# Pins, load order and an operand's copy at three places of a one-core attention and routing kernel

## The chip, the cores and the metric

The kernel runs on one core of one Trainium2 chip. The metric is the device time of one execution in microseconds (us). Several executions were timed, and one more was taken with the hardware profiler; the profile shows the span of that execution on the core, which is a little shorter than its device time.

## The reference

Two blocks follow each other. The first is a linear attention with product features, for 4 batches, 4 heads, 1088 positions and a head dimension of 32:

```python
def phi(x):
    a = np.einsum('rd,bhsd->bhsr', S1, x)
    b = np.einsum('rd,bhsd->bhsr', S2, x)
    return np.einsum('bhsi,bhsj->bhsij', a, b).reshape(*x.shape[:-1], r * r)
q_p, k_p = (phi(q), phi(k))
num = np.einsum('bhsf,bhfd->bhsd', q_p, np.einsum('bhsf,bhsd->bhfd', k_p, v))
den = np.einsum('bhsf,bhf->bhs', q_p, np.sum(k_p, axis=2))[..., None] + 1e-06
x = num / den            # to (4352, 128): all batches and positions, all heads
```

The second sends x (4352 tokens of 128) through 8 experts, weighted by a balanced routing matrix:

```python
P = np.exp(x @ w_gate - max)
for _ in range(8):
    P /= P.sum(1, keepdims=True) + 1e-09
    P /= P.sum(0, keepdims=True) + 1e-09
    P *= N / E
for e in range(E):
    out += P[:, e:e + 1] * (np.maximum(x @ w1[e], 0.0) @ w2[e])   # F = 1024
```

All arithmetic is in float32.

## The kernel before, in words

The experts' products are nearly all of the work, and they keep TensorE (PE) busy from the first tokens on. The program lists the work as items, each an expert `e` on a group of tokens. An item is cut into blocks, and each block has first products (x by W1, L1136 or, in the later form, L1302), a relu on ScalarE (ACT), sums on VectorE (DVE) and second products (relu by W2, L1590). Sums of operands replace some products: early items use seven products where eight would be needed (`seven`, L1215), and from item `first_new` on ("new" items) the first products use sums of x halves and W1 halves and the second ones use twenty products for four blocks (`twenty`, L1265).

Four stages follow one another.

- Up to about 115 us the attention of batches 0 to 3 runs. Early expert products are put between its steps (`fill`, L1702). For each batch `over` (L542) leaves a result in a tile `xt`, and `take_over` (L553) moves it: one transfer into a DRAM tile `xd` (L556) and four from there into `xT`, the tokens for the experts (L558). For the last batch it is called twice: L626 moves columns 0 to 192 over the POOL queue, L641 the rest over the SP queue. `logits` (L566) is the first that needs all of x.
- Beside it and beside the routing, `forms_ahead` (L267) prepares two forms of W1 for each later expert in DRAM tiles `wl` and `wf`: loads over SP (L265, L279), sign changes on ACT (L282, written in place in `turn`), sums by accumulating transfers over POOL (L276) and stores over SP (L279). Every transfer of it is pinned with `keep_in_program_order`.
- The routing (L668) runs to about 175 us. Then comes the turn to the new items: `join_halves` (L860) sums x halves by transfers over POOL (L865), `raw_second` (L803) loads W2 for the first new item, `first_weights` (L787) fetches the forms of W1 over SP (L793), and `make_second` builds the forms of W2 (`ws`, L238 on DVE, L241 on ACT).
- 68 blocks of new items (34 items of two) follow, one every 8.83 us, then the last group of seven-product items and the final sums (`last_part`, L979) with their stores (L1080).

What sets the order. The blocks `tc.manual_schedule` at L1710, L1734 and L1764 hold the named engines in the order in which the program is written: DVE, PE and ACT in the first and third, DVE and PE in the second. SP and POOL are not named, so their instructions are put in order by a scheduler at compile time, by when each is expected to be ready. `keep_in_program_order` ties one instruction behind the one written before it on the same engine. The attention stands in the block of L1734, the routing and everything later in that of L1764.

The order around the turn is written by hand: `TAIL` (L1599) names for each step of the last two old items what is called there. The tiles of W1 and W2 forms come from rings of two buffers with the tags "w1" and "w2" (`wpool`, L77), and the halves in `first_second_forms` (L778) from the ring "y" of a pool that is opened at L1771. In `first_product` (L1307) `wf` is taken as a list of two halves where `loaded_w` holds one. A dictionary `second_forms` decides in `first_weights` whether both forms are fetched or the first alone:

```python
if j in second_forms:
    parts = (0,)
...
if j in second_forms:
    loaded_w[j].append(second_forms[j])
```

At the very end `last_products` (L1245) gives the order of the last second products: products p2 and p4 of the last eight blocks were held back in `held`, and one product `(both, f, 2, 0, 0)` adds the upper and the lower half of the tile `f`, a copy of the sum s0, into the sum s2. `last_part` makes that copy when s0 is done (`k == 0`).

Of the kernel before, what the change touches and what calls it, by code (L numbers as in the profile page):

```python
# [44 lines left out]
def kernel(  # L45
# [12 lines left out]
    nc = tc.nc  # L58
    P = nc.NUM_PARTITIONS
    B, H, S, D = q.shape  # L60
# [58 lines left out]
    xT = big.tile([P, N + 2 * 32], F32, name="xT")  # L119

    W9 = 9 * 32
# [231 lines left out]
    both = consts.tile([P, H2], F32, name="both")  # L353
# [186 lines left out]
    turned = {}  # L540
# [11 lines left out]

    def take_over(b, lo, hi, queue):  # L553

        xd = dram.tile([P, H, hi - lo], F32, name=f"xd{b}{lo}")
        queue.dma_start(out=xd, in_=turned[b][:, :, lo:hi])  # L556
        for h in range(H):
            queue.dma_start(  # L558
                out=xT[32 * h:32 * (h + 1), b * S:b * S + 4 * W9].rearrange("d (f n) -> d f n", f=4)[:, :, lo:hi],
                in_=xd.rearrange("(f d) h n -> h d f n", f=4)[h])  # L560

    def logits(c):
        lo, hi = chunks[c]
# [38 lines left out]
    def attention(b):  # L602
# [22 lines left out]
        if b + 1 == B:  # L625
            take_over(b, 0, 192, nc.gpsimd)  # L626
# [9 lines left out]
        if b + 1 < B:  # L636
            take_over(b, 0, W9, nc.gpsimd)
            if b + 2 == B:
                forms_of_two()
        else:  # L640
            take_over(b, 192, W9, nc.sync)  # L641
# [226 lines left out]
    first_new = first_weighted  # L868
# [38 lines left out]
    def put(y, lo, n, queues):  # L907
        b0, nb = lo // 32, n // 32
        yt = pools[0].tile([P, NT3 // 32, 32], F32, tag="yt", name="yt", bufs=3)[:, 0:nb, :]
        nc.vector.transpose(out=yt.rearrange("p b d -> p (b d)"), in_=y)  # L910
        store(yt, b0, b0 + nb, queues)

    def part(g, k):

        if g in DIRECT:
            lo, n, _, es, _ = groups[g]
            nc.scalar.copy(kept[es[0]][:, lo + k * n:lo + (k + 1) * n], sums[g][k])
        elif groups[g][2] == 3 or PLAIN - 2 <= g < PLAIN:
            ended[k] = g
        elif g < len(groups) - 1:  # L920
            part_of_seven(g, k)
        else:
            last_part(g, k)
# [47 lines left out]
    def last_rooms(g):  # L971
        n = groups[g][1]
        own = parts.setdefault(g, {})
        if not own:
            own.update(y=[room("m")[:, n * t:n * (t + 1)] for t in range(2)],
                       **{a: room(a, n) for a in "zwxfr"})
        return [own[a] for a in "yzwxfr"]

    def last_part(g, k):  # L979


        lo, n, *_ = groups[g]
        s0, s1, s2, s3 = sums[g]

        def add(out, a, b):
            nc.vector.tensor_tensor(out, a, b, op=Alu.add)

        (y1, y2), z, w, x, f, r = last_rooms(g)
        if k == 3:
            nc.scalar.copy(r[upper], s3[lower])  # L990
            add(w[upper], s3[upper], r[upper])
        elif k == 0:
            nc.scalar.copy(z[upper], s0[lower])
            nc.scalar.copy(f, s0)
            add(x[upper], z[upper], w[upper])
            add(z[upper], x[upper], s0[upper])
        elif k == 2:
            nc.scalar.copy(r[lower], s2[upper])
            nc.scalar.copy(x[lower], s0[lower])
            add(y2[upper], z[upper], s2[upper])  # L1000
            add(y2[lower], s2[lower], r[lower])
            add(x[upper], x[upper], s2[upper])
            put(y2, lo + n, n, (nc.sync, nc.scalar))
        else:
            add(y1, s1, x)
            put(y1, lo, n, (nc.sync, nc.scalar))
# [175 lines left out]
    two_ = pqg[:, 0:2]  # L1182
# [32 lines left out]
    def seven(k):  # L1215

        j, q = blocks[k]
        _, w2, ws = loaded_w[j]
        h, ts, _ = hs[k]
        lo, hi = slice(0, H2), slice(H2, DM)  # L1220
        p1 = (w2[:, 2 * q, lo], h[0], 0, 0, 0)

        five, six = (0, 2) if weighted_of(k) else (2, 0)
        p6 = (ws[:, 1, q], ts[2], six, 1, 0)
        p2 = (w2[:, 2 * q + 1, lo], h[2], 1, 0, 0)
        p4 = (w2[:, 2 * q + 1, hi], ts[3], 1, 1, 0)
        p3 = (ws[:, 3, q], h[3], 2, 0, 0)
        p5 = (ws[:, 0, q], ts[0], five, 1, 0)
        p7 = (ws[:, 2, q], ts[1], 3, k % 2, 0)
        bank0 = [p1, p5] if five == 0 else [p1, p6]  # L1230
        bank2 = [p3, p6] if six == 2 else [p3, p5]
        if k >= len(blocks) - HELD:
            held.append([(k, p2), (k, p4)])
            if k == len(blocks) - 2:
                return bank0, bank2, [p7]
            if k == len(blocks) - 1:
                return [p7, p1], [p5, p3], [p6]
            return (bank0, bank2, [], [p7]) if k % 2 == 0 else (bank0[::-1], bank2[::-1], [], [p7])
        if k % 2 == 0:
            return bank0, [p2, p4], bank2, [p7]  # L1240
        return bank0[::-1], [p4, p2], bank2[::-1], [p7]

    held = []

    def last_products():  # L1245

        k = len(blocks) - 2
        one, two_ = ([[(b, p) for p in ps] for ps in seven(b)] for b in (k, k + 1))
        f = last_rooms(len(groups) - 1)[4]
        return one + held[:2] + two_ + held[2:4] + [[(k + 1, (both, f, 2, 0, 0))]] + held[4:]  # L1250

    SEEDED = {1: slice(0, P), 2: lower, 3: upper}

# [317 lines left out]
    def into(g, w, x, i, s, place, row=None):  # L1571
# [21 lines left out]
        if c == per:  # L1593
# [4 lines left out]

    TAIL = {12: ((weigh_half, first_new, 0), (raw_second, first_new, "ws4")),  # L1599
            13: ((copy_half, first_new, 0), (weigh_half, first_new, 1)), 14: ((copy_half, first_new, 1),),  # L1600
            15: ((join_halves, first_new), (first_weights, first_new)),
            16: ((first_second_forms, first_new), (weigh_half, first_new + 1, 0)),
            18: ((copy_half, first_new + 1, 0),), 20: ((weigh_half, first_new + 1, 1),),
            21: ((evacuate, 0),), 22: ((copy_half, first_new + 1, 1), (join_halves, first_new + 1)),
            23: ((evacuate, 1),)}
# [4 lines left out]
    def steps():  # L1610
# [13 lines left out]
        for k in ks:  # L1624
# [10 lines left out]
            if k == len(blocks):  # L1635
                for i, ps in enumerate(last_products()):
                    todo.setdefault(t + i, []).extend(ps)
# [171 lines left out]
```

## Time and profile before

| what | us |
| --- | --- |
| median of 3 runs | 891.15 |
| lowest and highest of them | 888.5, 895.88 |
| the profiled execution | 889.28 |
| span of the profiled execution | 887.5 |
| PE busy in the span | 876.1 |
| DVE, ACT, POOL busy in the span | 792.3, 570.3, 176.6 |

How to read the profile's lines. A group or an instruction is named by its line in the kernel (L1302), its engine and its operation, then output<-input by the program's tile names with their sizes. PE is the matmuls, PEld the loading of weights; SPq is the DMA issues of the SP queue, whose time is the issuing alone and not the transfer. A line of a timeline begins with the start in us from the span's start and the duration; instructions of the same kind that follow on one another are merged (x4). In square brackets stands how long the engine stood idle before it, and what it waited for. A list of waits has for each pair the total, how often, and the longest. "a" and "s" are tiles of accumulators, hx and hb relu outputs and their sums, xe and de the weighted x halves and their sums.

### The profile page before, as it was taken

The numbers are of one execution on the slowest core, as the hardware profiler recorded it, in microseconds if no ns is written. First come the engines' busy times: TensorE is split into PE (matmuls) and PEld (weight loads), VectorE is DVE, ScalarE is ACT, GpSimd is POOL, SyncE is SP. The second block draws the span as 40 slices with busy tenths as digits, with TensorE's granted clock in tenths as the row PEclk, the third lists the DMA queues.
The fourth block names the chain that finished last, engine by engine and source line by source line (L and its number), as shares of the span: only waits on it lengthen the run. The fifth ranks groups of instructions, "written<-read, shape, count | busy, mean of one in ns | idle before, by whom it ended". The sixth has DMA issues, their size and how long they took to land.

```text
span 887.5 us, 28700 instructions
## 1 busy us (share of the span) xinstructions
PE 876.1 (99%) x11790; PEld 626.4 (71%) x11790; DVE 792.3 (89%) x1628; ACT 570.3 (64%) x1309; POOL 176.6 (20%) x244
## 2 busy tenths in 40 slices
PE   8999999999999999999999999999999999999997
PEld 6777544454777777777787878787778777776665
DVE  7678779978999999999999999999998999998875
ACT  3446577677667677667676766666766666765543
POOL 3121433120221212222122211231122122200000
PEclk9999999999999999999999999999999999999999
DMA  9998899466877777876787777687568776774340
GB/s 247 299 278 283 175 209 217 114 166 173 252 221 228 234 202 211 250 185 200 189 249 177 203 210 200 167 242 216 174 167 229 211 221 182 208 199 96 96 102 13
DMA packets 97603, 175.19 MB, mean 197 GB/s; under 512 B 29232, under 2 KB 68992, under 8 KB 92624
## 3 DMA queue, kind: packets, MB, share of 16 engines
q1 hardware_dynamic: 74976, 140.20, 50.0%
q0 software_dynamic: 21264, 33.00, 21.6%
q8 instruction: 93, 1.52, 0.7%
q10 hardware_dynamic: 1232, 0.16, 0.1%
q14 instruction: 38, 0.31, 0.1%
HBM read 126.23 MB, written 25.08 MB: 170 GB/s over the span
## 4 chain that ended last, share of the span: by engine, by line
PE 84%; DMA 6%; DVE 6%; issue 2%; ACT 1%; SPq 1%; POOL 0%; DVEq 0%; POOLq 0%; ACTq 0%
PE s L1590 37%; PE a L1302 35%; PE a L1136 9%; DMA kx<-in_k_dram 2%; DVE hb L1204 1%; DMA ph<-kp 1%; DMA ph<-in_moe_w_dram 1%; PE a L532 1%; PE a L417 1%; DMA w<-wf 1%; DVE hx L1204 1%; DVE ws L238 1%; DMA v<-in_moe_w_dram 1%; DMA ws<-in_moe_w_dram 1%; DMA rb<-in_moe_w_dram 1%
## 5 line engine op out<-in xcount | busy, mean ns | idle before, releaser
L1302 PE MATMUL a<-xe,w 64*64 64x384 f32 x2180 | 420.8, 484 | 0.0
L1590 PE MATMUL s<-hb,ws 64*64 64x256 f32 (+4 forms) x2962 | 382.9, 384 | 0.5 <-DVE hx L1342 0.2
L1590 PE MATMUL s<-hx,ws 64*64 64x256 f32 (+1 forms) x2894 | 351.1, 377 | 0.1
L1302 PE MATMUL a<-de,w 64*64 64x384 f32 x1632 | 315.4, 483 | 0.7 <-DMA w<-wf 0.7
L1590 PEld LDWEIGHTS s<-hb,ws 64*64 64x64 f32 (+1 forms) x2962 | 201.8, 134 | 74.4 <-issue 25.7
L1590 PEld LDWEIGHTS s<-hx,ws 64*64 64x64 f32 (+1 forms) x2894 | 196.2, 133 | 56.2 <-issue 11.9
L1204 DVE TENSOR_TENSOR hb<-hb 128x512 f32<-128x512 f32 (+1 forms) x340 | 187.3, 576 | 1.3 <-ACT hb L1337 1.1
L1302 PEld LDWEIGHTS a<-xe,w 64*64 64x64 f32 x2180 | 147.2, 133 | 24.3 <-issue 1.4
L1337 ACT ACTIVATE hx<-a 128x384 f32<-128x384 f32 x204 | 97.0, 492 | 64.5 <-PE a L1302 62.7
L1337 ACT ACTIVATE hb<-a 128x384 f32<-128x384 f32 x204 | 97.4, 491 | 60.1 <-PE a L1302 57.2
L1136 PE MATMUL a<-xT,w 128*64 128x256 f32 (+3 forms) x576 | 130.4, 454 | 0.0
L1302 PEld LDWEIGHTS a<-de,w 64*64 64x64 f32 x1632 | 112.6, 133 | 22.0 <-issue 2.1
L1204 DVE TENSOR_TENSOR hx<-hx 128x512 f32<-128x512 f32 (+1 forms) x204 | 118.0, 593 | 0.4 <-ACT hx L1337 0.4
L865 POOL DMA_DIRECT2D de<-xe x68 | 56.5, 972 | 292.3 <-ACT de L858 187.1
L1140 ACT ACTIVATE hb<-a 128x256 f32<-128x256 f32 (+3 forms) x148 | 66.5, 452 | 54.4 <-PE a L1136 43.7
L1333 ACT ACTIVATE hb<-a 128x384 f32<-128x384 f32 x136 | 66.7, 490 | 34.6 <-PE a L1302 33.5
L1342 DVE TENSOR_TENSOR a<-a,hb 128x384 f32<-128x384 f32 x136 | 76.5, 563 | 11.0 <-PE a L1302 5.8
L1331 ACT COPY a<-a 128x384 f32<-128x384 f32 x136 | 63.0, 463 | 30.5 <-PE a L1302 30.0
L1155 DVE TENSOR_TENSOR hb<-hb 128x416 f32<-128x416 f32 (+7 forms) x90 | 60.7, 675 | 18.3 <-ACT hb L1140 15.3
L1136 PEld LDWEIGHTS a<-xT,w 128*64 128x64 f32 x576 | 55.7, 137 | 27.5 <-issue 16.2
L1590 PE MATMUL s<-hb,w 128*64 128x256 f32 (+3 forms) x280 | 69.8, 435 | 0.0
L865 POOL DMA_DIRECT2D de<-de x34 | 29.6, 872 | 138.9 <-issue 81.7
(222 smaller groups left out, 1005.5 us busy)
## 6 DMA issues: line engine op xcount, KB each, us to landing
ws<-ws SPq DMA_DIRECT2D x34, 1280.0 KB, 6.4
w<-wl SPq DMA_DIRECT2D x34, 512.0 KB, 7.7
w<-wf SPq DMA_DIRECT2D x34, 512.0 KB, 8.3
px<-pT SPq DMA_DIRECT2D x34, 384.0 KB, 9.2
w<-in_moe_w_dram SPq DMA_DIRECT2D x16, 512.0 KB, 5.0
de<-xe POOLq DMA_DIRECT2D x34, 192.0 KB, 3.1
de<-de POOLq DMA_DIRECT2D x34, 192.0 KB, 8.1
ws<-in_moe_w_dram SPq DMA_DIRECT2D x7, 512.0 KB, 8.0
```

The lines of the kernel that those rows point to most:

```text
L238: nc.vector.tensor_tensor(ws[:, c:c + len(ns)], blocks(x), blocks(y), op=Alu.subtract if off else Alu.add)
L865: tc.keep_in_program_order(nc.gpsimd.dma_start(out=out, in_=x, accum_op=Alu.add))
L1136: nc.tensor.matmul(ph[sl], loaded_w[j][0][:, P * f + H2 * s:P * f + H2 * (s + 1)], sources[j][:, lo:hi], start=True, stop=True, tile_posit ...
L1140: last_relu[:] = [nc.scalar.activation(out=out, in_=ph, func=Act.Relu).ins.name]
L1155: nc.vector.tensor_tensor(out, a, b, op=Alu.subtract)
L1204: nc.vector.tensor_tensor(places(out), places(a), places(b), op=Alu.subtract if off else Alu.add)
L1302: nc.tensor.matmul(out[sl], w[r, c0 + H2 * s:c0 + H2 * (s + 1)], x[r], start=start, stop=stop, tile_position=(H2 * row, H2 * s), skip_grou ...
L1331: witness(k, p, 1, nc.scalar.copy(b, bx))
L1333: witness(k, p, 5, nc.scalar.activation(out=m5s[p], in_=b, func=Act.Copy, scale=1.0 if p else -1.0))
L1337: ins = nc.scalar.activation(out=out, in_=x, func=Act.Relu)
L1342: ins = nc.vector.tensor_tensor(by if what == 1 else raw(k, p, 1, 1), bb[p], m5s[p], op=Alu.add)
L1590: mm = nc.tensor.matmul(sums[g][i][H2 * s:H2 * (s + 1), n * place:n * (place + 1)], w, x, start=c == (2 if t == 3 and row is None else 1) ...
```

## The change

Three edits. The first pins the transfers of the last batch's x, on POOL and on SP, with `keep_in_program_order`. The second calls `first_second_forms` for the first new item at step 15 of `TAIL`, ahead of `join_halves` and `first_weights`, where it was called at step 16 after them. The third is at the end: the product with `f` goes ahead of one more held pair (`held[3]`), and the two copies of `k == 0` on ACT change places, so that `f` is copied first.

```diff
     def take_over(b, lo, hi, queue):
 
+        def moved(out, x):
+            ins = queue.dma_start(out=out, in_=x)
+            if b + 1 == B:
+                tc.keep_in_program_order(ins)
+
         xd = dram.tile([P, H, hi - lo], F32, name=f"xd{b}{lo}")
-        queue.dma_start(out=xd, in_=turned[b][:, :, lo:hi])
+        moved(xd, turned[b][:, :, lo:hi])
         for h in range(H):
-            queue.dma_start(
-                out=xT[32 * h:32 * (h + 1), b * S:b * S + 4 * W9].rearrange("d (f n) -> d f n", f=4)[:, :, lo:hi],
-                in_=xd.rearrange("(f d) h n -> h d f n", f=4)[h])
+            moved(xT[32 * h:32 * (h + 1), b * S:b * S + 4 * W9].rearrange("d (f n) -> d f n", f=4)[:, :, lo:hi],
+                  xd.rearrange("(f d) h n -> h d f n", f=4)[h])
...
         elif k == 0:
+            nc.scalar.copy(f, s0)
             nc.scalar.copy(z[upper], s0[lower])
-            nc.scalar.copy(f, s0)
             add(x[upper], z[upper], w[upper])
             add(z[upper], x[upper], s0[upper])
...
-        return one + held[:2] + two_ + held[2:4] + [[(k + 1, (both, f, 2, 0, 0))]] + held[4:]
+        return one + held[:2] + two_ + held[2:3] + [[(k + 1, (both, f, 2, 0, 0))]] + held[3:]
...
-            15: ((join_halves, first_new), (first_weights, first_new)),
-            16: ((first_second_forms, first_new), (weigh_half, first_new + 1, 0)),
+            15: ((first_second_forms, first_new), (join_halves, first_new), (first_weights, first_new)),
+            16: ((weigh_half, first_new + 1, 0),),
```

## The prediction

> **What bounds the kernel now.** I read the first part of the page, then the list of what TensorE waited for, then the timelines of the three stages that the edits touch.
>
> ```profile
> span 887.5 us, 28700 instructions
> ...
> PE 876.1 (99%) x11790; PEld 626.4 (71%) x11790; DVE 792.3 (89%) x1628; ACT 570.3 (64%) x1309; POOL 176.6 (20%) x244
> ```
>
> TensorE (PE) is busy for 99% of the span: 11.4 us (887.5 - 876.1) is all that it stands idle, the start and the last outputs included. So an edit that removes no PE work can win only where PE stands. What PE waited for in the middle of the kernel, longest first (total, times, longest):
>
> ```profile
> PE a L566 <- DMA xT<-xd: 1.1, 1, 1.1
> PE a L1302 <- DMA w<-wf: 0.7, 1, 0.7
> ```
>
> The first row belongs to edit 1 (last batch's x), the second to edit 2 (second form of W1). Edit 3 (two products, two copies) lies at the end, where PE has run out of work and the last sums and stores are a chain of their own. The profiled execution took 889.28 us: its span and 1.78 us around it.
>
> **Edit 1: the last batch's moves pinned.** No instruction is added or removed; ten DMA issues get a tie. On SP (start, duration):
>
> ```profile
> 94.64 1.23 SPq L265 DMA_DIRECT2D wl<-in_moe_w_dram  x2
> ...
> 97.33 1.62 SPq L279 DMA_DIRECT2D kp<-in_moe_w_dram  x1
> ...
> 99.95 0.72 SPq L556 DMA_DIRECT2D xd<-xt  x1
> 100.76 0.63 SPq L279 DMA_DIRECT2D wf<-v  x1
> ...
> 105.39 1.74 SPq L558 DMA_DIRECT2D xT<-xd  x4
> 111.61 0.54 SPq L279 DMA_DIRECT2D wf<-kx  x1
> ```
>
> On POOL, and then PE, which waits for these moves:
>
> ```profile
> 96.33 1.19 POOL L556 DMA_DIRECT2D xd<-xt  x1
> ...
> 104.32 2.24 POOL L558 DMA_DIRECT2D xT<-xd  x4 [6.80 <-DMA xd<-xt]
> ```
> ```profile
> 109.52 1.50 PE L566 MATMUL a<-xT,wg 128*32 128x512 f32 x10 [1.12 <-DMA xT<-xd]
> ```
>
> In the code the SP move (L641) is written ahead of the form loads that the rows show before it (94.64 to 97.33) and inside it (100.76). Those loads are pinned already, yet they overtook the move. A pin ties an instruction to the one written before it on its engine. Between the move and the first of these loads one manual_schedule block ends and the next begins (L1734, L1764), and the rows show that the loads' chain of pins does not reach back over that border. The edit pins the moves backwards, to what stands ahead of them already; it ties no load to a move. On POOL the row of 104.32 already has the four xT issues on end behind their xd. So I expect both queues in the same order and a cost of 0. From the other side: if the loads did go behind the moves, the xd transfers would share the DMA engines with less, and at best the whole 1.12 us would go. A loss is bounded too: about nine issues of 0.6 us would move into SP's empty stretch from 107.13 (105.39 + 1.74) to 111.61, 5.4 us into 4.48, so the later forms would go about 1 us later; their readers wait until past 180. I take 0, bounds -1.12 and 0.
>
> **Edit 2: the second form of the first new item.** On SP, by the turn of the stage:
>
> ```profile
> 179.58 0.44 SPq L809 DMA_DIRECT2D ws<-in_moe_w_dram  x1
> 188.05 0.33 SPq L793 DMA_DIRECT2D w<-wl  x1
> 194.56 0.32 SPq L793 DMA_DIRECT2D w<-wf  x1
> 194.94 3.67 SPq L782 DMA_DIRECT2D y<-wf  x2
> ...
> 200.12 0.45 SPq L793 DMA_DIRECT2D w<-wl  x1
> 214.55 0.32 SPq L793 DMA_DIRECT2D w<-wf  x1
> 214.92 0.43 SPq L809 DMA_DIRECT2D ws<-in_moe_w_dram  x1
> ```
>
> Here the edit does more than reorder. Now first_weights runs first, finds no entry in second_forms and takes both forms; the second goes into a "w2" buffer that comes free at 194.5. Then first_second_forms fetches the same 512 KB once more into two "y" tiles, which nobody reads. With the order turned, first_weights finds the entry, takes w1 alone, and the products read the y tiles. So one issue of 512 KB (w<-wf at 194.56) is removed, of the 34 that the page lists (count, size, median us to landing), and the two y issues move ahead of w<-wl, into SP's empty stretch from 180.02 to 188.05. Their 3.67 us of issuing fits there.
>
> ```profile
> w<-wf SPq DMA_DIRECT2D x34, 512.0 KB, 8.3
> ```
>
> PE at this place:
>
> ```profile
> 200.00 0.86 PE L1302 MATMUL a<-xe,w 64*64 64x384 f32 x4
> 201.60 0.99 PE L1302 MATMUL a<-de,w 64*64 64x384 f32 x8 [0.74 <-DMA w<-wf]
> ...
> 203.04 0.43 PE L1590 MATMUL s<-hx,w 128*64 128x256 f32 x1
> ```
> ```profile
> DMA to landing us min/median/max: 8.2/8.2/8.2
> ```
>
> The last line is the landing of the two y loads: issued by 183.7 (180.02 + 3.67), they land by 191.9, 8.9 us before PE asks at 200.86. The wait of 0.74 us goes. What is late next: de, whose first sums were in by 194.04, since POOL's next step started on them, and hx for the product at 203.04, which would then come at 202.30.
>
> ```profile
> 194.04 0.87 POOL L865 DMA_DIRECT2D de<-de  x1 [4.19 <-DMA de<-xe]
> ```
> ```profile
> 200.54 1.61 DVE L1155 TENSOR_TENSOR hx<-hx 128x512 f32<-128x512 f32 x3
> ...
> 220.21 0.42 DVE L238 TENSOR_TENSOR ws<-ws 128x256 f32<-128x256 f32 x1 [0.25 <-DMA ws<-in_moe_w_dram]
> ```
>
> The last hx sum ends at 202.15, 0.15 us before 202.30, so the cover is thin but there. One item on, the w2 buffer that is no longer taken (free since 194.5) goes to the load that now waits from 200.57 to 214.55 for the other one. So this load, and the ws load behind it on SP, come up to 14 us earlier, and DVE's wait of 0.25 us at 220.21 goes as well; without that, DVE would stand there 0.99 us once PE is 0.74 ahead. The traffic stays about as large from 195 to 210: 1 MB (w<-wf and y) leaves it and 1 MB (the next w<-wf and ws) comes in. PE itself did not wait for that DVE stall, so I take -0.74, bounds 0 and -0.99.
>
> **Edit 3: the end.**
>
> ```profile
> 878.72 0.36 ACT L993 COPY z<-s 64x256 f32<-64x256 f32 x1
> 878.89 1.08 PE L1590 MATMUL s<-hb,w 128*64 128x256 f32 x8
> 879.11 0.37 ACT L994 COPY f<-s 128x256 f32<-128x256 f32 x1
> 879.22 0.42 DVE L986 TENSOR_TENSOR x<-z,w 64x256 f32<-64x256 f32 x1
> ...
> 879.76 0.38 PE L1590 MATMUL s<-f,both 128*64 128x256 f32 x1
> ...
> 879.77 0.42 DVE L986 TENSOR_TENSOR z<-x,s 64x256 f32<-64x256 f32 x1
> ...
> 880.39 0.37 ACT L998 COPY r<-s 64x256 f32<-64x256 f32 x1 [0.91 <-PE s L1590]
> ...
> 880.79 0.42 DVE L986 TENSOR_TENSOR m<-z,s 64x256 f32<-64x256 f32 x1 [0.59 <-ACT r L998]
> ```
>
> No work is added. The f product moves ahead of one pair of held products, four of the eight records of the row at 878.89, so about 0.43 us earlier (879.33). The f copy, now first, ends at 878.72 + 0.37 = 879.09, before that. So the r copy can start near 879.96 instead of 880.39. But the z copy ends 0.39 us later, at 879.47; with the same distances its sums start at 879.60 and 880.15, end at 880.57, and the m sum, 0.13 us behind, starts at 880.70 instead of 880.79. From there DVE works without a pause to the last store. I take -0.09. Bounds: -0.43 if z is not on that chain, +0.39 if r does not come earlier and all of z's delay stays.
>
> **The sum.** 889.28 + 0 - 0.74 - 0.09 = 888.45 us against the profiled execution, bounds 886.7 and 889.7. That execution lies below the median of the runs, 891.15 (888.5 to 895.88). The middle of the four executions is 890.2, and 0.83 us less is my prediction: **889.4 us**. Scatter of several us between runs is larger than the effect.
>
> **The rivals.**
> (a) The pins do put the loads behind the moves, and the logits' wait goes too: 889.4 - 1.1 = 888.3. For it: PE does wait for these moves. Against: pinned loads overtook them.
> (b) PE starts 0.74 us earlier and gives it back, because DVE sets the pace behind the turn: 889.4 + 0.74 = 890.1.
>
> ```profile
> 201.00:210.00 9.00, 8.40 (x72) 3.53 (x72) 6.81 (x19) 6.58 (x15) 1.73 (x2) 1.00 0.70 180
> ...
> 230.00:240.00 10.00, 9.91 (x149) 7.08 (x145) 9.44 (x22) 6.57 (x15) 3.37 (x4) 1.00 0.69 175
> 240.00:250.00 10.00, 10.00 (x151) 7.38 (x147) 10.00 (x24) 6.75 (x16) 1.73 (x2) 1.00 0.96 277
> ```
>
> The columns are the stretch and its length, then busy us of PE, weight loads, DVE, ACT and POOL. For it: DVE is busy 19.4 of 20 us from 230 to 250. Against: before that it has room, 6.81 of 9 us, and its work there starts when PE or ACT lets it.
> (c) On the other side: the y tiles' room comes free late, and their issue, now at the head of SP's queue, holds w<-wl. All that the trace says is that the room was free at 194.94. w<-wl is needed at 200.00, and L793's loads from 170 to 240 landed so long after their issue:
>
> ```profile
> DMA to landing us min/median/max: 4.0/6.4/7.1
> ```
>
> With the median and 0.44 us for each y issue (like the one at 179.58), PE loses what their start lies past 192.7 (200.00 - 6.4 - 0.88). It decides from 193.5 on, where the loss passes the saved 0.83. At the latest, 194.94 with the long 3.67 us issue, w<-wl lands at 205.0 and PE loses 5.0: 889.4 + 5.0 = 894.4. Against: neighbours from the same pool were writable at 179.58 (the ws4 tile).
> (d) PE's idle time hides most of what is lost at the turn, since weight loads there take 3.53 of 9 us against 7.38 of 10 at 240. If freeing SP's queue let 201 to 210 run at the later rate, it would need 9 x 0.39 / 0.74 = 4.8 us: 889.4 - 4.2 = 885.2. Against: PE shows no further wait there, and products over all 128 rows need fewer loads. (The Trainium skill, Perfetto Trace Analysis, section Identifying the Most-Contended Engine, says that matmul busy time is a poor measure of headroom and LDWEIGHTS busy share a better one; by it this rival would be the likeliest. The low share here agrees with it, while no row shows anything for PE to gain from these loads.)
>
> **How the numbers follow.** Forecast 0.66, (a) 0.08, (b) 0.17, (c) 0.06, (d) 0.03. The range reaches from the lowest run less 0.83 and 1.12, 886.5, to 892.7, half way from the median to the highest run less 0.83; it holds (a), (b), the nearer part of (c), and the runs' scatter. One per cent, 8.9 us, is about what a measurement of this kernel can tell from no change. Only scatter, or (d) with more than the 9 us reckoned, is faster by that, and only scatter on top of (c) slower: 0.02 and 0.03, and 0.95 for within 1%.
>
> **What would show it.** Edit 1 right: SP's order from 94 to 112 us unchanged and PE's wait at L566 still about 1.1 us; wrong if the four xT issues stand ahead of the form loads. Edit 2 right: y<-wf near 180, w<-wf one issue fewer, no wait of L1302 on wf, the next w<-wf directly behind w<-wl near 200, and every later period about 0.7 us earlier; wrong if PE waits for w<-wl or hx instead. Edit 3 right: f before z on ACT, the f product near 0.4 us earlier against its neighbours, the m sum hardly earlier. A result outside 886.5 to 892.7 without a difference in PE's waits would be scatter; with one, my sum is wrong.

## The result, and the profile after

| | median us (runs) | against before, 95% interval |
| --- | --- | --- |
| before, timed beside the change | 890.48 (22) | |
| the change | 887.92 (22) | 0.9976 [0.9964, 0.9987] |
| the change without its pins, timed another time (before 889.96) | 889.39 (12) | 0.9995 [0.9983, 1.0008] |

The change makes the kernel a little faster, by 2.1 us (1.2 to 3.2) in the first comparison, as the ratio has it (the two medians lie 2.56 us apart); the prediction had 0.83 us, which lies below that interval, and a time of 889.4 us, which lies in its own range of 886.5 to 892.7 as the 887.92 does. The third row has the same instructions in the same order on every engine as the second, so the two are two measurements of one program: they give -2.1 and -0.4 us, and their middle is a ratio of 0.9986, -1.3 us. Three more kernels below fetch the forms in the new order (`load`, `after_real`, `dve_z`); they give 0.9981 to 0.9984, 1.4 to 1.7 us faster than before. All of it is well within 1%.

The profiled execution of the change took 890.2 us, longer than the one of before (889.28). That is no contradiction: landmarks in the program tell where in the span the time goes, and here the change's delay lies ahead of the turn. The rows are, for the change, PE's first product of the turn, and on ACT the 5th, 8th, 44th and 45th of the 68 copies `de`, one per block of new items:

```profile
202.59 0.86 PE L1306 MATMUL a<-xe,w 64*64 64x384 f32 x4
203.28 0.88 PE L1306 MATMUL a<-de,y 64*64 64x384 f32 x8
```
```profile
218.04 0.53 ACT L862 COPY de<-xe 128x384 f32<-128x384 f32 x1
236.38 0.50 ACT L862 COPY de<-xe 128x384 f32<-128x384 f32 x1
555.63 0.50 ACT L862 COPY de<-xe 128x384 f32<-128x384 f32 x1
564.46 0.50 ACT L862 COPY de<-xe 128x384 f32<-128x384 f32 x1
```

The same copies of before:

```profile
216.41 0.53 ACT L858 COPY de<-xe 128x384 f32<-128x384 f32 x1
234.78 0.50 ACT L858 COPY de<-xe 128x384 f32<-128x384 f32 x1
554.02 0.50 ACT L858 COPY de<-xe 128x384 f32<-128x384 f32 x1
562.85 0.50 ACT L858 COPY de<-xe 128x384 f32<-128x384 f32 x1
```

The turn comes 2.59 us later in the change (202.59 against 200.00). It does not come from the edits: SP's `ws` issue ahead of the moved loads is 2.64 us later already (182.22 against 179.58), and up to there every engine has the same instructions in the same order in both. From there on the kernel before is 0.96 us slower by the 5th copy (16.41 us behind its turn against 15.45), 0.99 by the 8th, and 0.98 by the 44th and the 45th: what is lost there is not won back in these 360 us, and nothing is added. Reading a profile of this kernel from the turn, and not from its start, takes the scatter of the start away and makes differences of 0.02 us visible. The rest of this document is read so.

SP's queue at the turn, the change, answers to the rows of 179.58 to 214.92 in the prediction:

```profile
182.22 0.43 SPq L813 DMA_DIRECT2D ws<-in_moe_w_dram  x1
183.03 1.50 SPq L786 DMA_DIRECT2D y<-wf  x2
190.64 0.32 SPq L797 DMA_DIRECT2D w<-wl  x1
191.00 0.42 SPq L825 DMA_DIRECT2D px<-pT  x1
202.70 0.32 SPq L797 DMA_DIRECT2D w<-wl  x1
203.11 0.41 SPq L797 DMA_DIRECT2D w<-wf  x1
203.57 0.42 SPq L813 DMA_DIRECT2D ws<-in_moe_w_dram  x1
```
```profile
w<-wf SPq DMA_DIRECT2D x33, 512.0 KB, 8.5
```

The y loads stand in the gap, one `w<-wf` is gone (33 for 34), the products of `de` read `y` and wait for nothing (the row at 203.28 has no bracket), and the next item's `w<-wf` and `ws` follow `w<-wl` at once, 0.5 to 1.0 us behind the turn, where they came 14.6 and 14.9 us behind it.

At the end, the change (ACT, DVE and PE in order of time):

```profile
879.90 0.36 ACT L994 COPY r<-s 64x256 f32<-64x256 f32 x1 [1.79 <-PE s L1594]
880.29 0.43 DVE L990 TENSOR_TENSOR w<-s,r 64x256 f32<-64x256 f32 x1 [1.05 <-ACT r L994]
880.33 0.37 ACT L997 COPY f<-s 128x256 f32<-128x256 f32 x1
880.73 0.36 ACT L998 COPY z<-s 64x256 f32<-64x256 f32 x1
880.94 0.38 PE L1594 MATMUL s<-f,both 128*64 128x256 f32 x1
881.12 0.42 DVE L990 TENSOR_TENSOR x<-z,w 64x256 f32<-64x256 f32 x1 [0.40 <-ACT z L998]
881.57 0.37 ACT L1002 COPY r<-s 64x256 f32<-64x256 f32 x1 [0.48 <-PE s L1594]
881.65 0.42 DVE L990 TENSOR_TENSOR z<-x,s 64x256 f32<-64x256 f32 x1
882.17 0.43 DVE L990 TENSOR_TENSOR m<-z,s 64x256 f32<-64x256 f32 x1
884.56 0.45 DVE L914 STREAM_TRANSPOSE yt<-m 128x256 f32<-128x256 f32 x1
```

Before, the first of these r copies stood at 878.29 and the last transpose at 883.17. From the one to the other it is 4.66 us in the change and was 4.88: 0.22 us won. The m sum no longer waits for ACT's second r copy (no bracket); z's sums now come last.

### The profile page after: what moved, and what is told of

Its sections match the earlier page's. It is cut to its first block, busy times and chain, and to the rows that moved or that the text cites. A ratio compares the mean times of both kernels' runs of the same rounds, so it can differ in the third digit from the quotient of the medians.

```text
span 888.4 us, 28700 instructions
## 1 busy us (share of the span) xinstructions
PE 877.8 (99%) x11790; PEld 625.5 (70%) x11790; DVE 792.9 (89%) x1628; ACT 570.4 (64%) x1309; POOL 176.6 (20%) x244
## 4 chain that ended last, share of the span: by engine, by line
PE 88%; DVE 5%; DMA 4%; SPq 1%; issue 1%; ACT 0%; DVEq 0%
PE s L1594 39%; PE a L1306 36%; PE a L1140 11%; DMA qx<-in_q_dram 1%; DVE hb L1208 1%; DMA kx<-in_k_dram 1%; DMA qb<-qab 1%; DVE hx L1208 1%; DVE ws L238 1%; PE a L532 1%; DMA v<-in_v_dram 1%; DMA xd<-xt 1%; PE a L417 1%; DVE hb L1159 0%; DVE a L1346 0%
## 5 line engine op out<-in xcount | busy, mean ns | idle before, releaser
L1594 PE MATMUL s<-hb,ws 64*64 64x256 f32 (+4 forms) x2962 | 382.4, 384 | 0.5 <-DVE hx L1346 0.2
L1594 PE MATMUL s<-hx,ws 64*64 64x256 f32 (+1 forms) x2894 | 351.1, 376 | 0.1
L1306 PE MATMUL a<-de,w 64*64 64x384 f32 x1600 | 309.6, 483 | 0.0
L1594 PEld LDWEIGHTS s<-hb,ws 64*64 64x64 f32 (+1 forms) x2962 | 201.4, 133 | 75.1 <-issue 26.4
L1594 PEld LDWEIGHTS s<-hx,ws 64*64 64x64 f32 (+1 forms) x2894 | 196.2, 133 | 56.6 <-issue 11.9
L1594 PE MATMUL s<-hb,w 128*64 128x256 f32 (+3 forms) x280 | 69.1, 435 | 0.0
```

The lines of the kernel that those rows point to most:

```text
L1306: nc.tensor.matmul(out[sl], w[r, c0 + H2 * s:c0 + H2 * (s + 1)], x[r], start=start, stop=stop, tile_position=(H2 * row, H2 * s), skip_grou ...
L1594: mm = nc.tensor.matmul(sums[g][i][H2 * s:H2 * (s + 1), n * place:n * (place + 1)], w, x, start=c == (2 if t == 3 and row is None else 1) ...
```

## The experiments

Each kernel is the one before with the edit shown, unless another kernel is named; lines of an edit that are left out are marked by `...`. Each ratio is against the kernel before as it was timed beside that run. The line numbers are those of the change (+4 from L566 on; `after_real` 7 more). In the texts on record "r copy" is the first of the two r copies of the last group (L994). This table comes from their profiles, and the paragraphs refer to it. "wf" and "ws" are the us from issue to landing of the turn's late `w<-wf` and of the second item's W2 load; "turn", "2nd item" and "later" are what the kernel lies behind the change at the 5th, 8th and 45th `de` copy, counted from its own turn; then the us from the r copy to the last transpose and from there to the end of the span.

| kernel | wf | ws | turn | 2nd item | later | r to yt | yt to end | ratio |
| --- | --- | --- | --- | --- | --- | --- | --- | --- |
| before | 6.9 | 5.3 | 0.96 | 0.99 | 0.98 | 4.88 | 4.33 | |
| before_again | 5.8 | 5.4 | 0.00 | 0.15 | 0.15 | 4.89 | 4.37 | 1.0001 [0.9985, 1.0018] |
| before_third | 7.2 | 5.5 | 1.27 | 1.50 | 1.68 | 4.88 | 4.23 | |
| pins | 4.8 | 5.7 | 0.01 | 0.47 | 0.48 | 4.88 | 4.45 | 0.9993 [0.998, 1.0007] |
| end | 5.3 | 5.1 | 0.00 | 0.01 | 0.31 | 4.67 | 4.19 | 0.9996 [0.9983, 1.001] |
| swap | 5.0 | 5.5 | 0.01 | 0.28 | 1.41 | 4.88 | 4.13 | |
| product | 5.9 | 5.6 | 0.00 | 0.36 | 1.59 | 4.71 | 4.60 | |
| no_dead | 5.7 | 5.7 | 0.01 | 0.43 | 0.44 | 4.87 | 3.85 | 0.9986 [0.9975, 0.9997] |
| load_full | | | 0.00 | 0.01 | 0.18 | 4.88 | 4.34 | 0.9994 [0.9981, 1.0007] |
| load | | | 0.00 | 0.01 | 0.02 | 4.88 | 3.84 | 0.9982 [0.9966, 0.9998] |
| the change | | | 0 | 0 | 0 | 4.66 | 3.84 | 0.9976 [0.9964, 0.9987] |
| no_pins | | | 0.00 | 0.01 | 0.02 | 4.65 | 3.79 | 0.9995 [0.9983, 1.0008] |
| after_real | | | 0.01 | 0.01 | 0.06 | 4.65 | 3.83 | 0.9984 [0.9964, 1.0004] |
| dve_z | | | 0.00 | 0.01 | 0.02 | 5.09 | 3.80 | 0.9981 [0.9972, 0.9991] |

**pins**: the ten pins alone.

```diff
+        def moved(out, x):
+            ins = queue.dma_start(out=out, in_=x)
+            if b + 1 == B:
+                tc.keep_in_program_order(ins)
...
```

> Edit 1 alone: the last batch's moves pinned, the old turn and the old end. Theory A (each edit works only where it stands): the pins tie the moves to nothing that they had not already stood behind, so 0 us against before (within 0.1 percent), PE's wait for xT in the trace still between 1 and 2 us, SP with the form loads ahead of xd. Theory C (the pins put the moves ahead, and part of the 2.1 us comes from there): 0.5 to 1.1 us faster, form loads behind the xT issues. Theory B (the wait for wf at the turn varies from execution to execution and was small, 0.74, in the profile of before): PE's wait on wf in this profile differs from 0.74 by more than 0.5; theory A: 0.5 to 1.0.

Measured: 889.15 us, ratio 0.9993 [0.998, 1.0007]. Every engine has the instructions of before in the same order, so the edit does nothing, as forecast. That its profile shows no wait of the turn for `wf` is therefore not the pins' work: it is the first sign that the wait comes and goes between executions of one program.

**load**: the order of the loads alone.

```diff
-            15: ((join_halves, first_new), (first_weights, first_new)),
-            16: ((first_second_forms, first_new), (weigh_half, first_new + 1, 0)),
+            15: ((first_second_forms, first_new), (join_halves, first_new), (first_weights, first_new)),
+            16: ((weigh_half, first_new + 1, 0),),
```

> Edit 2 alone: second form fetched into the y tiles first, no w2 buffer taken. Theory A: no wait on wf; from the first x product of the turn (L1302, 200.00 before) to the last r copy (L990, 878.29 before) 677.3 us instead of 678.3, so 0.9 to 1.1 us faster in time. Theory B: the same stretch, but about 2 us faster in time, since most executions of before wait longer than the profiled one.

Measured: 887.82 us, ratio 0.9982 [0.9966, 0.9998], so 1.6 us faster (0.2 to 3.0), an interval that holds both theories' times. From the turn to the r copy it is the change to 0.01 us (677.32 and 677.31 us, against 678.29 before).

**end**: the copies and the product alone.

```diff
+            nc.scalar.copy(f, s0)
             nc.scalar.copy(z[upper], s0[lower])
-            nc.scalar.copy(f, s0)
...
-        return one + held[:2] + two_ + held[2:4] + [[(k + 1, (both, f, 2, 0, 0))]] + held[4:]
+        return one + held[:2] + two_ + held[2:3] + [[(k + 1, (both, f, 2, 0, 0))]] + held[3:]
```

> Edit 3 alone: the two copies swapped and the f product one pair earlier. Theory A: from the last r copy (L990) to the end of the span 8.5 to 9.0 us instead of 9.2; in time 0.2 to 0.7 us faster, which rounds can hardly tell from 0; turn as before with a wait of 0.5 to 1.0 us on wf. Theory B: a wait on wf in this profile that differs from 0.74 by more than 0.5.

Measured: 888.87 us, ratio 0.9996 [0.9983, 1.001], no measurable difference. In the trace the last transpose comes 0.21 us earlier behind the r copy (4.67 against 4.88). This execution, with the old order of the loads, lost next to nothing at the turn (0.01), where before had lost 0.96: as theory B said, the wait for `wf` changes between executions.

**after_real**: the whole change, with SP's form loads really put behind the last batch's moves by a tie that reaches over the border of the two schedule blocks (the edit is to the change).

```diff
-            tc.keep_in_program_order(nc.sync.dma_start(out=out, in_=x))
+            ins = tc.keep_in_program_order(nc.sync.dma_start(out=out, in_=x))
+            if last_move:
+                tc.add_manual_dep(ins.ins, last_move.pop(), mybir.DependencyInfo(
+                    mybir.DependencyClass.NoSync, mybir.DependencyReason.DATA), reason="behind the last move")
...
+                if queue is nc.sync:
+                    last_move[:] = [ins.ins.name]
```

> The changed kernel, and in addition the first form load written after the moves tied behind the last of the xT issues on SP, so that xd and the four xT issues really go ahead of them. Rival (a) of the prediction: the xd transfer shares less, xT lands earlier, PE's wait at the logits goes from 1.1 to 1.5 us down to under 0.3, and the time is 1 to 1.5 us below the changed kernel's. The other possibility: POOL's own xd, issued 3 us earlier and beside the same loads, still lands late and the wait stays at 0.7 us or more, so the gain is under 0.5 us; or the later forms come late and ACT waits for them, no gain or a loss.

Measured: 888.64 us, ratio 0.9984 [0.9964, 1.0004], not faster than the change. The moves themselves did get faster: POOL's `xT` issues waited 3.48 us for `xd`, where those of the change waited 7.09 (the change's row first).

```profile
105.23 2.24 POOL L556 DMA_DIRECT2D xT<-xd  x4 [7.09 <-DMA xd<-xt]
```
```profile
102.44 2.24 POOL L561 DMA_DIRECT2D xT<-xd  x4 [3.48 <-DMA xd<-xt]
```

PE waits 0.8 us for `xT`, where the change waits 1.5; but the other executions, without the tie, have 0.6 to 2.6, so one profile can't say that this wait became shorter. The forms come later, and in PE's list of waits the row of `hb` has grown from 0.2 (L1594 in the change) to 0.9, and the one at L718 is new:

```profile
PE s L1601 <- DVE hb L1166: 0.9, 2, 0.7
PE a L577 <- DMA xT<-xd: 0.8, 1, 0.8
...
PE a L718 <- ACT hb L1151: 0.4, 1, 0.4
```

Over the first 200 us the rows of PE's list add up to 5.4 us, against 5.5 in the change, and the turn comes at 202.41 against 202.59. No gain from rival (a)'s order shows.

**no_dead**: the kernel before without the two y loads that nobody reads.

```diff
-            16: ((first_second_forms, first_new), (weigh_half, first_new + 1, 0)),
+            16: ((weigh_half, first_new + 1, 0),),
```

> The kernel before without the two y loads that nobody reads; the second W1 form is still asked for at its old place and still takes the w2 buffer. Theory A (the wf wait at the turn comes from the late issue at 194.6 us, when the buffer comes free): the wait of about 0.7 us stays wherever it showed, first turn product to last r copy stays 677.7 to 678.3 us, ratio 1.000. Theory B (it comes from the 512 KB of dead y loads that share the DMA engines with it): the wait is gone, the load lands well ahead of PE, first turn product to last r copy is 677.3 to 677.7 us, ratio 0.999 to 0.9995, and most of what the full edit gained at the turn is had without moving anything.

Measured: 888.87 us, ratio 0.9986 [0.9975, 0.9997]. `wf` landed in 5.7 us, among the 4.8 to 5.9 that other executions have with the y loads beside it, so whether these loads are what delays it in some executions is not settled. What the traces do show is that in the two executions with the late `wf` the loads beside it were slow too: there the two y issues took 3.67 and 3.72 us and landed in 8.2 and 8.6, against 0.95 to 2.71 and 5.5 to 6.2 in the other five with the old order. The turn lost nothing, but 0.43 us were lost in the second item: on SP, `ws` was still asked for 14 us behind the turn (213.49), and DVE waited:

```profile
219.18 0.42 DVE L238 TENSOR_TENSOR ws<-ws 128x256 f32<-128x256 f32 x1 [0.64 <-DMA ws<-in_moe_w_dram]
```

Yet it is measurably faster than before. The table shows a reason that nobody had expected: from the last transpose its end is 0.5 us shorter.

**load_full**: the y loads first and read, as in the change, with the spare form still loaded into the w2 buffer (the edit is to `load`).

```diff
-        if j in second_forms:
-            parts = (0,)
...
-            loaded_w[j].append(second_forms[j])
+            loaded_w[j][1] = second_forms[j]
```

> The y loads go first and the first item's products read them, as in the change, but the w2 buffer is still taken and filled with the same form, so that the second item's second form and the ws load behind it stay near 214.5 us. Theory A (the gain is PE's wait for wf alone): first turn product to last r copy as in the change, 677.3 us, no wait of the turn on wf. Theory C (a part comes from the buffer that is left free, through DVE's wait for the ws load near 220 us): the wf wait is gone but the stretch is 677.6 to 677.8 us, and the DVE wait for ws stands as before with about 0.25 to 1 us. Whole time 0.998 by A, 0.999 by C.

Measured: 888.75 us, ratio 0.9994 [0.9981, 1.0007]. Nothing is lost at the turn. It doesn't test theory C, though: the spare form has no reader, its buffer is free as soon as it has landed, and the second item's `w<-wf` came at 201.19, not at 214.5. What it does tell: with as many loads on SP as before, the end is as long as before (4.34), with the rest as in `load` (3.84).

**swap** and **product**: the two halves of the edit at the end, each alone (one profile each; the diffs are the two parts of that of `end`).

> Only the two copies swapped (f before z), the products as before. Theory E1 (the x sum waits for the z copy, as the prediction had it): the last r copy comes at its old distance, the z copy 0.39 us later, x and the m sum up to 0.39 us later, r copy to last transpose 5.0 to 5.3 us. Theory E2 (before, x waits for the w sum on DVE and not for z): x starts about 0.25 us later at most, the m sum waits for r anyway, and r copy to last transpose stays 4.9 us within 0.1. No gain by either.

> Only the f product moved one pair of products earlier, the copies as before (z, then f). By E1 and E2 alike the f copy still ends at about 0.76 us behind the z copy's start, just where the f product now wants to start, so the product comes 0.3 to 0.43 us earlier or waits for f by about 0.05 to 0.1 us; the r copy about 0.35 us earlier in absolute terms. E1: z's own chain is not delayed, so the m sum comes up to 0.4 us earlier and this half alone is better than the whole edit at the end by up to 0.3 us. E2: x is held by the w sum, and the m sum by z at r + 2.5 us, so the end moves by 0.1 to 0.3 us, the same as the whole edit within 0.1.

Measured: r copy to last transpose 4.88 us for the swap and 4.71 for the product, against 4.88 before and 4.66 for both. The swap delays z and costs nothing (E2); the product earlier gives 0.17, and both 0.22. E1, which was the prediction's way to see it, is refuted by both. What the swap is for shows in the second r copy, which waits for the f product: it comes 2.10 us behind the first one before and in the swap, 1.93 in the product alone, where the f copy still goes second, and 1.67 with both. In these two executions over 1.1 us were lost about 355 us behind the turn, which is no work of these edits:

```profile
555.67 0.43 PE L1594 MATMUL s<-hx,ws 64*64 64x256 f32 x2 [0.83 <-DMA ws<-ws]
```

(swap; a `ws<-ws` load, 1280 KB of W2 forms from DRAM, was 9.0 us under way there.) The same load took 7.0 us in before and 7.6 in the change, without a loss. Over all fourteen executions, landings of up to 7.8 us go with a loss of at most 0.04 there, 8.1 or 8.2 with 0.16 to 0.30, and 9.0 and 9.2 with 1.1 and 1.2.

**before_again**, **before_third**: the kernel before, unchanged. **no_pins**: the change without its pins.

> The kernel before unchanged, as a control. Its ratio to itself should be 1.000 with an interval of about 0.0015 to each side; a ratio as far off as 0.998 would say that a part of the change's measured 2.1 us is chance. Theory M (each execution with the old order loses something at the turn, 0.3 to 1.0 us, through the wait for wf or, without it, DVE's wait for the ws load): from the first turn product to the end of the second new item it comes 0.3 to 1.0 us behind the change. Theory O (the loss is only an occasional wait): most executions lose nothing there, as the one with the end alone did.

> The same kernel once more, for one more profile. Theory M: again 0.3 to 1.0 us lost in the first 35 us behind the turn; theory O: 0 or nearly so. Near 360 us behind the turn a second loss, 0 to 1.2 us in the executions so far, is expected with either order of the loads, as its wait is for weights asked for at the same time in all.

> The whole change without the ten pins, which by the order of the instructions is the same program as the change. Theory M and O alike: 0.00 us lost at the turn, no wait on wf or on the ws load, last r copy to last transpose as in the change, 4.65 us; ratio the same as the change within the intervals, 0.9975 to 0.999. If the pins did something, it is slower than the change.

Measured: the control gives 1.0001 [0.9985, 1.0018]; before_third's one run took 891.46 us; no_pins 889.39 us and 0.9995 [0.9983, 1.0008], a little under its expected gain. At the turn before_third lost 1.27 us and before_again nothing, then 0.23 and 0.15 in the second item. PE's and DVE's waits in before_third:

```profile
203.46 0.99 PE L1306 MATMUL a<-de,w 64*64 64x384 f32 x8 [1.05 <-DMA w<-wf]
```
```profile
222.28 0.42 DVE L238 TENSOR_TENSOR ws<-ws 128x256 f32<-128x256 f32 x1 [0.45 <-DMA ws<-in_moe_w_dram]
```

On average M holds rather than O, but only three of seven losses lie within its 0.3 to 1.0 us: over the seven executions with the old order the loss by the second item is 0.99, 0.15, 1.50, 0.47, 0.01, 0.28 and 0.36 us, on average 0.54, which seven values as scattered as these give to about 0.2 us; over the six in which the y loads come first and are read it is at most 0.01.

**dve_z**: no_pins, with the z copy on DVE ahead of the w sum.

```diff
-            add(w[upper], s3[upper], r[upper])
         elif k == 0:
             nc.scalar.copy(f, s0)
-            nc.scalar.copy(z[upper], s0[lower])
+            nc.vector.tensor_copy(z[upper], s0[lower])
+            add(w[upper], s3[upper], r[upper])
```

> The whole change without the pins, and the z copy of the end moved from ScalarE to VectorE ahead of the w sum, where VectorE stood idle for 1.05 us. If s0 is complete by then (E2, the z chain sets the end in the change): x no longer waits 0.40 us for z, the m sum comes 0.17 to 0.3 us earlier and is held by the r copy, last r copy to last transpose 4.4 to 4.5 us. If s0 is not complete until just before the f copy, the copy starts near the r copy's end and delays the w sum: 4.65 us or up to 0.4 us more. Whole time within 0.3 us of the run without it, under what the measurement can tell.

Measured: 888.21 us, ratio 0.9981 [0.9972, 0.9991]. The end became longer, 5.09 us for 4.65: DVE's copy began only when ACT's copy of the same sum (878.24 to 878.61) was through, though the sum was complete when that one began, and it pushed the w sum behind it. Why the two copies did not overlap is not shown.

```profile
878.65 0.42 DVE L997 COPY z<-s 64x256 f32<-64x256 f32 x1 [1.49 <-ACT f L996]
```

It is no version that beats the change; that its ratio is nominally better than that of no_pins shows how little such ratios can tell.

## Why the prediction was right or wrong

**Edit 1, taken at 0: right, by its own reason.** SP's order from 94 to 112 us is the old one and PE still waits for `xT`. SP's timeline of the change, and a row of its list of what PE waited for:

```profile
95.26 1.23 SPq L265 DMA_DIRECT2D wl<-in_moe_w_dram  x2
...
101.50 0.58 SPq L556 DMA_DIRECT2D xd<-xt  x1
102.17 0.59 SPq L279 DMA_DIRECT2D wf<-v  x1
...
106.24 1.75 SPq L556 DMA_DIRECT2D xT<-xd  x4
112.44 0.54 SPq L279 DMA_DIRECT2D wf<-kx  x1
```
```profile
PE a L570 <- DMA xT<-xd: 1.5, 1, 1.5
```

**Edit 2, taken at -0.74: the mechanism right, the step to its size wrong.** The prediction took the one wait that its profile showed as a constant of the kernel, and set aside DVE's wait for `ws` with "PE itself did not wait for that DVE stall". The runs show both waits as what is left over when a landing time, which differs from execution to execution, exceeds a fixed slack. `w<-wf` is issued 5.44 us ahead of the turn's first product and asked for 0.69 behind it (the change's rows): 6.13 us of slack. Landings of 4.8 to 5.9 us cost nothing, 6.9 and 7.2 cost 0.96 and 1.27, about 0.2 more than they exceed the slack by. `ws` is issued 13.96 us behind the turn, plus what PE has lost there (14.92 and 15.23 us in the two executions with the late `wf`), since the load ahead of it on SP waits for a buffer that PE's products set free (in before, SP waited 13.9 us for PE there). Its landings of 5.1 to 5.7 us left DVE waits of 0 to 0.69 us at L238, and in each of the seven executions that show such a wait, PE lost it less 0.21 or 0.22 us: 0.25 cost 0.03, 0.36 cost 0.15, 0.45 cost 0.23, and 0.69 cost 0.47. So DVE's stall does reach PE, beyond about 0.2 us of cover. The prediction's profile, with 0.25, lay just at that edge, and its step "without that, DVE would stand there 0.99 us once PE is 0.74 ahead" does not hold: a PE that is earlier has the `ws` load issued earlier too, and the two losses simply add up (1.27 and 0.23 in before_third). On average the turn lost 0.54 us before, both waits together, less than the 0.74 taken and the bound of 0.99. With the loads early nothing is lost.

Inside that, the wait's row itself was too small a price. It shows 0.74 us, and by the 5th `de` copy the kernel was 0.96 later. The first two products of the turn start 1.60 us apart before (200.00 and 201.60) and 0.69 apart in the change (202.59 and 203.28): 0.91. PE normally starts the next product before the modelled end of the one ahead (0.69 against 0.86), and idle time is counted only from that end. The Trainium skill, Perfetto Trace Analysis, section Tensor Engine Instruction (MATMUL, LD_WEIGHTS), says the same of the end: it is estimated from the instruction's size and not observed. The 0.17 us between 0.91 and 0.74 agree with it: they are the 0.86 less the 0.69. The last 0.05 us to 0.96 are not traced.

**Edit 3, taken at -0.09: the right sign, the step "z's sums follow the z copy at the same distance" wrong.** It gave 0.22. In the profile of before, x did not wait for the z copy (ended 879.08) but for the w sum on its own engine, which ended at 879.12:

```profile
878.69 0.43 DVE L986 TENSOR_TENSOR w<-s,r 64x256 f32<-64x256 f32 x1 [1.05 <-ACT r L990]
```

x started 0.93 us behind the r copy there and 1.22 in the change: 0.29 later, not 0.39, and z's sum then followed after 0.53 us instead of 0.55. The m sum came 2.27 us behind the r copy, before 2.50; the prediction had 2.41. The f product came 0.43 us earlier, as forecast.

**What the prediction had no term for: the very end, -0.5 us.** From the last transpose to the end of the span it is 4.13 to 4.60 us in the eight executions with before's number of loads on SP (mean 4.33) and 3.79 to 3.85 in the six with 512 KB fewer, `no_dead` among them and `load_full` not. Two rows of SP's timeline and the landings of the last eight stores, first of before and then of the change:

```profile
883.64 0.32 SPq L1080 DMA_DIRECT2D out_dram<-yt  x1
884.29 0.32 SPq L1080 DMA_DIRECT2D out_dram<-yt  x1
```
```profile
DMA to landing us min/median/max: 1.7/1.9/2.3
```
```profile
885.03 0.32 SPq L1084 DMA_DIRECT2D out_dram<-yt  x1
885.39 0.46 SPq L1084 DMA_DIRECT2D out_dram<-yt  x1
```
```profile
DMA to landing us min/median/max: 1.6/1.8/1.9
```

The last store follows the third after 0.65 us before and 0.36 in the change, and the slowest landing shrinks by 0.4. The longer distance, 0.65 to 0.67, stands in seven of the eight; in `load_full` the pause stands ahead of the third store instead, 1.25 us behind the first for 1.04; none of the six has it. Removing the loads does it; why a load taken out near 194 us moves a pause of SP's queue at 884 us stays open.

**The sum.** -0.54 at the turn, -0.22 and -0.50 at the end make -1.26 us, beside 0.83 predicted, and beside -1.3 us as the middle of the two measurements. That 0.83 came as near as it did is in part luck: the turn was taken 0.20 too large, the copies 0.13 too small, and the 0.50 of the very end had no term. The range says less still about the mechanism, since single runs of the change alone scatter from 886.59 to 890.2. The first measurement's 2.1 us is not fully traced: its interval begins at 1.2. The late `ws<-ws` landing near 355 us behind the turn cost 0.4 us on average in the seven executions of the old order and under 0.1 in the six others, but the load is asked for at the same place in both, and whether that difference is more than chance stays open.

**The rivals.** (a) did not occur, and in after_real, where its order was made, no gain shows. (b), the gain given back by DVE, is refuted: from the 8th copy on the distances stay within 0.02 us until the 44th in every kernel. (c), a late y tile: refuted, the issue came at 183.03 and `w<-wl` stood 11.95 us ahead of the turn in both. (d), weight loads at the later rate, is refuted too: the stretch that answers to 201 to 210 us (span, PE, weight loads, DVE and so on) has the low share as before,

```profile
203.59:212.59 9.00, 9.00 (x84) 3.60 (x80) 7.28 (x19) 6.58 (x15) 1.73 (x2) 1.00 0.91 254
```

3.60 us of 9 against 3.53. By what the Trainium skill says on headroom (Perfetto Trace Analysis, Identifying the Most-Contended Engine: LDWEIGHTS busy share rather than matmul busy share) this stretch had room; the 4.2 us that the prediction worked out for it did not come.

## What to carry to other kernels

A DMA wait in one profile is one draw: work out the slack between issue and use, compare it with the spread of landing times, and price the wait as an average over executions, with the stalls behind it counted too. Compare profiles from a landmark inside the program and not from the start, and time a change of one part in a thousand twice before its size is believed. A load that nobody reads is worth removing for its own sake.

## What the runs showed of the hardware that was not expected

- The same 512 KB load at the same place of the program landed in 4.8 to 7.2 us (eight executions), and a 1280 KB one in 7.0 to 9.2 (fourteen); both ranges cross the point from which PE waits.
- The start scatters more than all edits together: the turn came between 198.66 and 203.66 us in fourteen executions. PE's wait for `xT` ahead of it was 0.6 to 2.6 us.
- With 512 KB of loads fewer on SP's queue near 194 us, the last store's issue, 690 us on, came 0.29 us sooner behind the third, and the end of the kernel became 0.5 us shorter (3.79 to 3.85 us in six executions against 4.13 to 4.60 in eight).
